# The order of all tasks of a fused threshold attention and quick-GELU kernel, sought anew with other ranks

## The chip, the cores and the metric

The kernel runs on one core of one Trainium2 chip. The metric is the device time of one launch in microseconds, taken as the median of the runs shown.

## The reference

Eight batches of eight heads, 576 positions, 64 values a head; the attention's result is laid out as 4608 tokens of 512 values and goes through a feed-forward block with 2048 hidden values. The two weight matrices come as 64-bit floats, the rest as 32-bit ones.

```python
scores = scale * np.matmul(q, k.transpose(0, 1, 3, 2))
thresh = np.max(scores, axis=-1, keepdims=True) - tau
scores = np.where(scores >= thresh, scores, -1000000000.0)
scores = scores - np.max(scores, axis=-1, keepdims=True)
attn = np.exp(scores)
attn = attn / (np.sum(attn, axis=-1, keepdims=True) + 1e-09)
attn_out = np.matmul(attn, v)
x = attn_out.transpose(0, 2, 1, 3).reshape(B * S, H * D)
h = x @ w_in
g = h * (1.0 / (1.0 + np.exp(-1.702 * h)))
out = (g @ w_out).astype(np.float32)
```

## The kernel before

Two heads of one batch make a pair; there are 32 pairs, n = 0 to 31, and four of them make a batch. The work is cut into named tasks, written (n) or (n, part) below.

For one pair: `load_qk` (L410) and `load_v` (L422) bring q, k and v in through SP's queue. `prep` (L522, DVE) turns q and k. `scores` (L538, PE, nine parts in PSUM), and `keep` (L555, ACT) copies each part to SBUF. `in_groups` (L561, DVE, five parts, the last of half the size) and `over_tiles` (L570) take the maxima; `over_halves` (L581, L594) and `turn_rows` (L605) make one row of limits, which goes to DRAM with `row_out` (L651) and comes back spread over all partitions with `row_in` (L660); pair 2 spreads it on DVE (`spread_max`, L642). `sub` (L666, DVE, five parts), `mask` (L672, ACT) and `exps` (L676, ACT) turn the scores into weights. `values` (L687, PE) multiplies them with v. The sums of the weights are made on PE for pairs 0 to 4 (`sums_by_pe` L687, `one_row` L718, `spread_sums` L770 and L772) and on DVE from pair 5 on (`in_groups` with add, `turn_sums` L744 to L749, then the DRAM trip `sums_out`, `sums_in`). `place_x` (L789, DVE) divides and writes the feed-forward's input xT.

The weights come in 32 pieces of 1 MB, piece 0 to 15 of w_in and 16 to 31 of w_out, each by two transfers on POOL's queue (`load_w`, L473 and L474), one piece after the other. DVE and ACT turn a piece into 32-bit floats by integer work: `cv_ex` (L484, DVE), `cv_power` (L492, ACT), `cv_frac` (L498 and L502, DVE), `cv_end` (L510, DVE). A piece is loaded into one of four corners of the room of w_out or one of two buffers; the next piece for that place is loaded after `cv_end` of the one before. The first load also waits for `hold(3)` (L529), a POOL copy that waits for `prep(3, 1)`.

The feed-forward works on 18 blocks of 256 tokens. Blocks 0 and 1 go together: 32 tasks `mm1_0(j, i)` (L844, PE; j = 0 to 15 slices of the hidden values, i the block), of which slices 4x to 4x+3 need pieces 4x to 4x+3 of w_in, each slice followed by `tanh` (L813, ACT) and `gelu_0` (L850, DVE), which frees one of two PSUM banks; then 32 tasks `mm2(i, p)` (L826, PE), where p = 0 to 7 needs pieces 16+2p and 17+2p. Blocks 2 to 13 take a first product at L804, `gelu` at L816 and a second at L995 by seven products of half size; blocks 14 to 17 do both products so (L909, L995).

What sets the order: nothing in the code's sequence does. Every task is handed to `task(engine, cost, rank, f, ...)`, with the tasks it comes after, the buffers it takes and gives back, and a cost in us. `run_in_order` then plays all of it at build time, engine by engine: an engine that is free takes the ready task of the lowest rank, and the instructions are written in the order in which tasks are taken. The chip runs each engine's list strictly in that order. The rank is the pair's number plus a bias by the kind of task: table EARLY for pairs 0 to 3, SECOND for 4 to 7, LATER for the rest, CV for the weight tasks. FIRST (-9.0) is the rank of the feed-forward's work on ACT, DVE, POOL and SP and of transfers; LAST (1000.0) is that of the feed-forward's products on PE. From pair 7 on, `values` of pair n-2 and `scores` of pair n are bound together, part by part; a pair's scores are let in after every 16th feed-forward task (`gate`).

Of the kernel before, what the change touches and what calls it, by code (L numbers as in the profile page):

```python
# [30 lines left out]
def kernel(  # L31
# [97 lines left out]
    for x in ("raw0", "raw1", "qkT0", "qkT1", "mb"):  # L129
# [3 lines left out]


    EARLY = {
        "exps": -17.61,
        "in_groups": 12.77,
        "keep": 26.48,
        "load_qk": 6.42,
        "load_v": 0.46,  # L140
        "mask": 4.73,
        "one_group": -15.86,
        "one_row": -9.06,
        "over_halves": -11.42,
        "over_tiles": -0.06,
        "place_x": -9.61,
        "prep": -11.56,
        "row_in": 31.26,
        "row_out": -12.68,
        "scores_run": 26.41,  # L150
        "spread_max": 4.27,
        "spread_sums": 4.87,
        "sub": 8.56,
        "sums_by_pe": -5.69,
        "sums_in": 2.27,
        "sums_out": 16.51,
        "turn_rows": -16.86,
        "turn_sums": -5.4,
        "values": 24.67,
        "w_sum": 2.1,  # L160
        "x_sum": -20.63,
    }
    SECOND = {
        "exps": -12.92,
        "in_groups": 29.73,
        "keep": 6.19,
        "load_qk": 1.9,
        "load_v": 13.07,
        "mask": 1.29,
        "one_group": 2.55,  # L170
        "one_row": -2.79,
        "over_halves": -24.79,
        "over_tiles": 9.26,
        "place_x": -19.31,
        "prep": -22.42,
        "row_in": -9.56,
        "row_out": -26.33,
        "scores_run": 2.45,
        "spread_max": 6.39,
        "spread_sums": -1.67,  # L180
        "sub": 27.62,
        "sums_by_pe": 38.88,
        "sums_in": 16.9,
        "sums_out": 8.98,
        "turn_rows": 12.04,
        "turn_sums": -0.33,
        "values": 2.02,
        "w_sum": -3.88,
        "x_sum": -12.22,
    }  # L190
    LATER = {
        "exps": 1.49,
        "in_groups": 1.97,
        "keep": -9.78,
        "load_qk": -5.98,
        "load_v": -3.59,
        "mask": 21.95,
        "one_group": 4.78,
        "one_row": -20.84,
        "over_halves": 8.94,  # L200
        "over_tiles": -3.1,
        "place_x": 4.68,
        "prep": -7.1,
        "row_in": 2.23,
        "row_out": -2.52,
        "scores_run": -13.43,
        "spread_max": -3.68,
        "spread_sums": -27.9,
        "sub": 9.4,
        "sums_by_pe": 4.28,  # L210
        "sums_in": 8.55,
        "sums_out": -0.12,
        "turn_rows": -4.72,
        "turn_sums": 8.12,
        "values": 0.63,
        "w_sum": 21.55,
        "x_sum": 7.65,
    }
    CV = {
        "cv_end": -26.29,  # L220
        "cv_ex": 6.34,
        "cv_frac": -13.49,
        "cv_power": -9.91,
        "load_w": 3.03,
    }

    LAG = {"PE": 0.26, "DVE": 0.18, "ACT": 0.22, "POOL": 0.18, "SP": 0.1}
# [118 lines left out]
    TWICE = ()  # L346
# [728 lines left out]
    SHARED = 0.2 if BY_POOL else 0.0  # L1075
    FFU = 1.727
    T_RANK = FIRST

    W_RANK = (0, 15.75, 22.55, 26.06, 2.06, 16.74)
    ready_w, w_loads, w64 = [], [], 0  # L1080
    for i in range(len(pieces)):
        y = 0 if i < NDC else 2 if i < n_in else 4
        n = NDC if i < NDC else n_in - NDC if i < n_in else n_in
        first = (0, 0, NDC, 0, n_in)[y]
        rank = W_RANK[y] + (W_RANK[y + 1] - W_RANK[y]) * (i - first) / n
        if not wide:
# [12 lines left out]
        over = [ready_w[y] for y in range(i) if i >= n_in and stage(y) == (i - n_in) // PER_STAGE]  # L1099
        ready_w.append(task("DVE", 0.61 + SHARED, rank, cv_end, i, after=[a, m] + over, give=place))  # L1100
# [168 lines left out]
    exped, loaded, summed = {}, {}, {}  # L1269

    def valued(n, pv):

        nonlocal next_blk
        b, hp = divmod(n, NPAIR)
        new = {(b * S + x) // BLK for x in cuts(b)[:-1]} if hp == 0 else set()
        if b:
            new -= {(b * S - 1) // BLK}
        placed[n] = task(
            "DVE", 1.05, float(n), place_x, n, after=[summed[n], pv], take=("xT",) * len(new),
            give=("psA", "rc"),  # L1280
        )
        while hp == NPAIR - 1 and (next_blk + 1) * BLK <= (b + 1) * S:
            if next_blk >= TAIL:
                if (next_blk - TAIL) % 2:
                    two_blocks(next_blk - 1)
            elif next_blk >= PLAIN:
                feed_forward(next_blk)
            elif next_blk == PLAIN - 1:
                first_blocks()
            next_blk += 1  # L1290

    for n in range(NP):
        gate = per_pair * (n - LEAD)
# [38 lines left out]
        if n >= JOINT:  # L1332

            a = None
            for t in range(NKT + 1):
# [4 lines left out]
                    after=exped[m] + [loaded[m], pq, pk] + after if t == 0 else [a],  # L1340
                    take=("psA",) if t == 0 else (), give=(f"v_m{m % 2}",) if t == NKT else (),
# [5 lines left out]
                a = w  # L1347
                for j in js:
# [143 lines left out]
```

## Time and profile before

| what | before |
|---|---|
| time, median of 3 runs | 1314.48 us (1312.47 to 1315.28) |
| profiled execution: span of the instructions | 1309.8 us |
| busy PE | 1260.5 us (96%) |
| busy DVE | 1002.2 us (77%) |
| busy ACT | 646.6 us (49%) |
| DMA, mean over the span | 79 GB/s; 214 GB/s in the first 131 us |

The span runs from the first to the last instruction of one profiled execution; no time of its own is listed for that execution, so the span is set against the runs: 4.7 us of the median lie around it (2.7 of the fastest run, 5.5 of the slowest). Busy times of different engines overlap. Numbers in the page's slices are tenths of 1/40 of the span, 32.7 us each. The traced task times below are read from the instructions of an engine in order, which are the planner's tasks in order.

### The profile page before, as it was taken

Reading aid. Unit: us, or ns where it says so; the run is one execution under the profiler, and the core shown is the slowest. Engines: PE = TensorE matmul, PEld = TensorE weight load, DVE = VectorE, ACT = ScalarE, POOL = GpSimd, SP = SyncE. Lnnn points to the kernel's source line nnn. Section 1 sums busy time; section 2 is a strip of 40 time slices with the busy share of each in tenths; the row PEclk is TensorE's granted clock in tenths of the full one; section 3 lists DMA queues with packets and bytes.
Section 4 is the critical chain, followed back from the end, with each engine's and each line's share of the span. In section 5 each row is a group of like instructions: output and inputs, shape, how many; then the busy total and the mean of one; then the engine's idle time right before and its main releaser. Section 6 shows DMA issues by size and latency. Waiting matters only on the chain. (4 is left out here: it accounts for less than half of the span.)

```text
span 1309.8 us, 22824 instructions
## 1 busy us (share of the span) xinstructions
PE 1260.5 (96%) x9128; PEld 972.6 (74%) x9128; DVE 1002.2 (77%) x1601; ACT 646.6 (49%) x830; POOL 246.1 (19%) x300
## 2 busy tenths in 40 slices
PE   5869999999999999999999999999999999999998
PEld 2436854477688777777778888777777778888887
DVE  7999998989998877778877877777888864652642
ACT  5975656766664544455554545454556540210210
POOL 1301210022030212112020302020212117120120
PEclk8989999999999999999999999999999999999999
DMA  6976967264322222221222222222122110000000
GB/s 118 339 186 214 282 209 132 67 125 83 82 57 71 55 64 64 56 57 44 63 47 61 55 71 55 72 56 70 42 52 54 38 44 9 9 1 33 1 1 32
DMA packets 194309, 103.78 MB, mean 79 GB/s; under 512 B 160284, under 2 KB 171292, under 8 KB 194204
## 3 DMA queue, kind: packets, MB, share of 16 engines
q1 hardware_dynamic: 180476, 64.30, 20.6%
q0 software_dynamic: 11360, 37.74, 9.7%
q8 instruction: 71, 1.16, 0.4%
q10 hardware_dynamic: 2368, 0.30, 0.2%
q14 instruction: 34, 0.28, 0.1%
HBM read 88.40 MB, written 9.70 MB: 75 GB/s over the span
## 5 line engine op out<-in xcount | busy, mean ns | idle before, releaser
L561 DVE TRANSPOSE_TENSOR_REDUCE part<-arena 128x36 f32<-128x1152 f32 x295 | 361.5, 1241 | 45.9 <-ACT arena L555 32.3
L804 PE MATMUL hps<-xT,w_in 128*128 128x256 f32 x1536 | 336.9, 380 | 0.4 <-DVE arena L816 0.4
L804 PEld LDWEIGHTS hps<-xT,w_in 128*128 128x128 f32 x1536 | 290.8, 190 | 45.5 <-issue 5.7
L672 ACT ACTIVATE arena<-arena 128x1152 f32<-128x1152 f32 (+1 forms) x160 | 169.4, 1058 | 144.9 <-DVE arena L666 144.6
L555 ACT COPY arena<-ps 128x576 f32<-128x576 f32 x288 | 170.4, 647 | 121.2 <-PE ps L538 120.9
L666 DVE TENSOR_TENSOR arena<-arena 128x1152 f32<-128x1152 f32 (+1 forms) x158 | 197.5, 1281 | 19.6 <-DMA arena<-row 19.5
L995 PE MATMUL ops<-w_out,arena 128*128 128x256 f32 x896 | 202.9, 381 | 1.2 <-DVE arena L816 1.1
L676 ACT ACTIVATE arena<-arena,shift,scl 128x1152 f32<-128x1152 f32 (+1 forms) x160 | 200.1, 1251 | 4.1
L538 PE MATMUL ps<-arena 64*64 64x288 f32 x2304 | 174.1, 419 | 25.1 <-DVE arena L522 14.4
L995 PEld LDWEIGHTS ops<-w_out,arena 128*128 128x128 f32 x896 | 169.0, 190 | 29.1 <-DVE arena L816 3.7
L961 POOL TENSOR_TENSOR arena<-arena 128x256 f32<-128x256 f32 x56 | 50.8, 907 | 658.4 <-DVE arena L816 556.7
L687 PE MATMUL pv<-arena 64*64 64x288 f32 x2176 | 161.2, 410 | 0.0
L538 PEld LDWEIGHTS ps<-arena 64*64 64x64 f32 x2304 | 83.7, 137 | 93.6 <-ACT arena L555 30.7
L995 PE MATMUL ops<-arena 128*128 128x256 f32 x672 | 150.6, 380 | 0.0
L813 ACT ACTIVATE th<-hps 128x512 f32<-128x512 f32 x112 | 66.0, 589 | 167.9 <-PE hps L804 148.2
L995 PEld LDWEIGHTS ops<-arena 128*128 128x128 f32 x672 | 127.3, 190 | 19.3 <-issue 2.2
L687 PEld LDWEIGHTS pv<-arena 64*64 64x64 f32 x2176 | 82.0, 135 | 55.3 <-issue 12.8
L1017 DVE SCALAR_TENSOR_TENSOR osb<-ops,osb 128x256 f32<-128x256 f32 x98 | 39.5, 414 | 91.8 <-PE ops L995 85.0
L816 DVE SCALAR_TENSOR_TENSOR arena<-th,hps 128x512 f32<-128x512 f32 x96 | 64.1, 667 | 37.1 <-ACT th L813 37.0
L844 PE MATMUL hps<-xT,w_in 128*128 128x256 f32 x256 | 57.3, 382 | 1.3 <-DVE arena L850 1.2
L826 PE MATMUL ops<-w_out,arena 128*128 128x512 f32 x128 | 56.4, 596 | 0.0
L844 PEld LDWEIGHTS hps<-xT,w_in 128*128 128x128 f32 x256 | 48.1, 190 | 11.0 <-DVE arena L850 3.0
(117 smaller groups left out, 1027.8 us busy)
## 6 DMA issues: line engine op xcount, KB each, us to landing
arena<-in_v_dram SPq DMA_DIRECT2D x128, 144.0 KB
arena<-in_q_dram SPq DMA_DIRECT2D x128, 72.0 KB
out_dram<-osb SPq DMA_DIRECT2D x36, 256.0 KB
arena<-in_k_dram SPq DMA_DIRECT2D x124, 72.0 KB
arena<-row SPq DMA_DIRECT2D x62, 144.0 KB
arena<-row_s SPq DMA_DIRECT2D x54, 144.0 KB
w_out<-in_moe_w_in_dram POOLq DMA_DIRECT2D x12, 512.0 KB, 9.4
arena<-in_moe_w_out_dram POOLq DMA_DIRECT2D x12, 512.0 KB, 5.9
```

Source lines behind the costliest of these rows:

```text
L538: nc.tensor.matmul(ps[ts(c, KT), h, 0:SH], lhsT=mats[n, 1][ts(h, D), ts(j, KT)], rhs=mats[n, 0][ts(h, D), ts(c, SH)], start=True, stop=True,)
L555: nc.scalar.copy(out=sT[n, t][:, u], in_=pss.pop((n, j))[:, :, 0:SH])
L561: nc.vector.tensor_reduce(out=stats[n, op][:, t * 2 * QB : min(2 * t + 2, NK) * QB], in_=sT[n, t].rearrange("p u h (g d) -> p (u h g) d", ...
L666: engine.tensor_tensor(out=s, in0=s, in1=mbs[n].unsqueeze(1).to_broadcast(list(s.shape)), op=ALU.subtract)
L672: nc.scalar.activation(out=s, in_=s, func=AF.Prelu, alpha=STEEP)
L676: nc.scalar.activation(out=s, in_=s, func=AF.Exp, scale=scl, bias=shift)
L687: nc.tensor.matmul(o[c][ts(h, D), 0:SH], lhsT=left(j, h)[ts(c, KT)], rhs=sT[n, t][ts(c, KT), u, h, :], start=(j == 0), stop=(j == NK - 1),)
L804: nc.tensor.matmul(hidden[j][:, ts(f, BLK)], lhsT=w_in[:, c, ds((f * HF + j) * P, P)], rhs=xTs[blk][:, c, :], start=(c == 0), stop=(c == N ...
L813: nc.scalar.activation(out=ths[j], in_=hidden[j], func=AF.Tanh, scale=GELU_SCALE / 2)
L816: nc.vector.scalar_tensor_tensor(out=g[:, :, j, :], in0=two(ths.pop(j)), scalar=1.0, in1=two(hidden.pop(j)), op0=ALU.add, op1=ALU.mult,)
L844: nc.tensor.matmul(hidden[j][:, ts(i, BLK)], lhsT=w_in[:, c, ts(j, P)], rhs=xTs[i][:, c, :], start=(c == 0), stop=(c == NDC - 1),)
L995: nc.tensor.matmul(banks[blk][k][:, ts(o, HM)], lhsT=left[:, j, :], rhs=right[:, j, :], start=(j == 0), stop=(j == HF - 1),)
```

## The change

All four bias tables get other values, and far larger ones: before they lie between -28 and +39, after between -55 and +218. Some kinds lose their entry where it isn't used. The bias now reaches tasks whose rank is negative as well (the loads of q and k of pairs 0 and 1), except those of rank FIRST and two tasks by name; before it reached ranks from 0 up. The ranks of the weight loads, W_RANK, change. Four costs that the planner reckons with change: `cv_frac` 0.95 to 1.05, `place_x` 1.05 to 0.9, `over_halves` of pairs that go by DRAM 0.8 to 1.05, `spread_sums` 1.05 to 1.15. No function that emits an instruction is touched.

```diff
     EARLY = {
-        "exps": -17.61,
-        "in_groups": 12.77,
...
-        "values": 24.67,
+        "exps": 142.34,
+        "in_groups": 132.24,
...
+        "values": 115.25,
...
     CV = {
-        "cv_end": -26.29,
-        "cv_ex": 6.34,
-        "cv_frac": -13.49,
-        "cv_power": -9.91,
-        "load_w": 3.03,
+        "cv_end": 53.64,
+        "cv_ex": 114.38,
+        "cv_frac": 162.71,
+        "cv_power": -13.03,
+        "load_w": 14.74,
     }
...
-        if 0 <= rank < LAST:
+        if rank != FIRST and rank < LAST and f not in (first_act, tau_terms):
             biases = EARLY if a[0] < NPAIR else SECOND if a[0] < 2 * NPAIR else LATER
...
-    W_RANK = (0, 15.75, 22.55, 26.06, 2.06, 16.74)
+    W_RANK = (10.13, -10.54, 49.5, -6.3, 43.87, 44.05)
...
-        a = task("DVE", 0.95 + SHARED, rank, cv_frac, i, after=[e])
+        a = task("DVE", 1.05 + SHARED, rank, cv_frac, i, after=[e])
...
-            "DVE", 1.05, float(n), place_x, n, after=[summed[n], pv], take=("xT",) * len(new),
+            "DVE", 0.9, float(n), place_x, n, after=[summed[n], pv], take=("xT",) * len(new),
...
-            "DVE", 1.05 if not quick else 1.3 if n in TWICE else 0.8, r, over_halves, n,
+            "DVE", 1.05 if not quick else 1.3 if n in TWICE else 1.05, r, over_halves, n,
...
-            summed[n] = task("DVE", 1.05, r, spread_sums, n, after=[a], take=("rc",))
+            summed[n] = task("DVE", 1.15, r, spread_sums, n, after=[a], take=("rc",))
```

What the order of the built instructions becomes, beside the order before:

- PE: six of the nine parts of pair 3's scores go between the sums and values of pair 1; the last three parts of pair 5's scores go behind `mm1_0(0, 0)` instead of ahead of it; `values(4)` and its sums go behind `mm1_0(14, 1)` instead of `mm1_0(13, 1)`; the block of `values(5)` and `scores(7)` goes ahead of `mm2(0, 7)` instead of behind `mm2(1, 2)`. From pair 8 on PE's list is the same but for one product of block 12.
- DVE: `prep` of pairs 2 and 3 earlier; `sub(1)` 8.4 us of work later and `sub(2)`, `sub(3)` 8.5 and 8.2 us of work earlier; `cv_end(0)` and `cv_end(1)` from before `sub(1, 2)` and `in_groups(2, 3)` to just ahead of `prep(4, 0)`; the sums of pair 5 and the maxima of pair 6 ahead of `cv_end(31)`.
- SP: the second `load_v` from before `load_qk(2)` to between `row_out(0)` and `row_in(0)`.
- POOL and ACT: the weight loads in the same order; single `keep` and `cv_power` tasks change places with `mask` and `exps`.

More of the change, by code (lines that the diff above doesn't have):

```diff
@@ L135 @@
     EARLY = {
-        "exps": -17.61,
-        "in_groups": 12.77,
[L138 to L158, printed above, removed]
-        "values": 24.67,
-        "w_sum": 2.1,
-        "x_sum": -20.63,
+        "exps": 142.34,
+        "in_groups": 132.24,
+        "keep": 118.26,
+        "load_qk": 114.85,
+        "load_v": 217.78,
+        "mask": 204.23,
+        "one_row": 151.17,
+        "over_halves": 77.78,
+        "over_tiles": 54.81,
+        "place_x": -28.9,
+        "prep": -36.6,
@@ L162 @@
+        "row_in": 119.13,
+        "row_out": 54.38,
+        "scores_run": -9.85,
+        "spread_max": -12.43,
+        "spread_sums": 67.21,
+        "sub": 12.03,
+        "sums_by_pe": -29.14,
+        "turn_rows": 99.41,
+        "values": 115.25,
+        "w_sum": -24.48,
     }
     SECOND = {
[L164 to L189, printed above, removed]
+        "exps": 14.77,
@@ new lines @@
+        "in_groups": 215.43,
+        "keep": 205.66,
+        "load_qk": 49.39,
+        "load_v": 15.49,
+        "mask": 201.87,
+        "one_row": 46.53,
+        "over_halves": 204.6,
+        "over_tiles": 205.68,
+        "place_x": 42.22,
+        "prep": 199.07,
+        "row_in": -16.08,
+        "row_out": -35.4,
+        "scores_run": 100.32,
+        "spread_sums": -22.91,
+        "sub": 212.9,
+        "sums_by_pe": 208.86,
+        "sums_in": -41.96,
+        "sums_out": 204.0,
@@ L190 @@
+        "turn_rows": -55.2,
+        "turn_sums": 98.03,
+        "values": 195.96,
     }
     LATER = {
[L192 to L217, printed above, removed]
+        "exps": 205.54,
+        "in_groups": 204.67,
+        "keep": -17.19,
+        "load_qk": 205.88,
+        "load_v": -16.08,
+        "mask": 217.32,
+        "over_halves": 69.93,
+        "over_tiles": -22.46,
@@ L218 @@
+        "place_x": 116.28,
+        "prep": 152.31,
+        "row_in": -55.43,
+        "row_out": 216.92,
+        "scores_run": -6.53,
+        "sub": 198.53,
+        "sums_in": -13.61,
+        "sums_out": 53.62,
+        "turn_rows": -6.06,
+        "turn_sums": 208.51,
+        "values": 194.66,
+        "x_sum": 204.79,
     }
     CV = {
-        "cv_end": -26.29,
-        "cv_ex": 6.34,
-        "cv_frac": -13.49,
-        "cv_power": -9.91,
-        "load_w": 3.03,
+        "cv_end": 53.64,
```

## The prediction

> **What bounds the kernel now.** I read the page first (busy times, slices), then the chain that ended last, then the windows, then the timelines of PE, DVE, SP and POOL.
>
> ```profile
> span 1309.8 us, 22824 instructions
> ...
> PE 1260.5 (96%) x9128; PEld 972.6 (74%) x9128; DVE 1002.2 (77%) x1601; ACT 646.6 (49%) x830; POOL 246.1 (19%) x300
> ...
> PE 16%; DVE 0%; issue 0%
> ```
>
> PE is busy 96% of the span, and the chain, followed back to 1091 us, is PE alone. The change emits the same instructions (9128 on PE), so the end is the sum of PE's work plus PE's idle time, and only the idle time can move. The windows say where it lies:
>
> ```profile
> core 0: us, PE busy (x) PEld busy (x) DVE busy (x) ACT busy (x) POOL busy (x), PEclk, DMA share, GB/s
> 0.00:131.00 131.00, 93.32 (x1087) 55.77 (x1088) 118.19 (x203) 91.03 (x117) 25.06 (x60) 0.91 0.75 214
> 131.00:262.00 131.00, 126.96 (x867) 75.69 (x869) 121.59 (x196) 84.32 (x105) 16.88 (x27) 0.99 0.66 172
> 262.00:1310.00 1048.00, 1040.26 (x7184) 841.14 (x7172) 762.43 (x1204) 471.23 (x610) 204.15 (x214) 1.00 0.21 51
> ```
>
> Of 49.3 us idle, 37.7 lie in the first 131 us, 4.0 in the next 131, 7.7 in the last 1048 (3.6 of them behind PE's last product). In the first 262 us DVE is busy 240 us; it idles 7.2 us at the start and hardly again, so there DVE is the bound and PE waits for it. The hinge is the first feed-forward product:
>
> ```profile
> 110.27 3.73 PE L538 MATMUL ps<-arena 64*64 64x288 f32 x32 [1.64 <-DVE xT L789]
> 113.93 6.39 PE L844 MATMUL hps<-xT,w_in 128*128 128x256 f32 x28
> ```
> ```profile
> 109.26 0.95 DVE L789 TENSOR_TENSOR xT<-pv,arena 128x256 f32<-128x256 f32 x4
> ```
>
> `place_x(3)` (L789) ends at 110.21; four score tasks then go first, and from 113.93 on PE has work without end. Later idle time is small: 1.2 us behind `gelu_0` (149 to 158), 2.44 us at 246.3 for a `keep`, under 1.1 us each after that.
>
> **The change part by part.** Unit costs are the steps from one start to the next on DVE in the first 400 us: `in_groups` 1.28 (last part 0.76), `sub` 1.30 (0.76), `prep` 0.68, `over_tiles` 0.44, `cv_ex` 0.34, `cv_frac` 1.09, `cv_end` 0.60, `turn_sums` 1.66.
>
> *Steady part and tail: nothing.* From `values(10)` on PE's list differs by one product that changes places with its neighbour, the last 193 feed-forward tasks are the same, and from pair 12 on `exps(n, 4)` stands at the same feed-forward task in both lists, 17 to 23 tasks of about 1.73 us ahead of `values(n)` up to pair 29. DVE and ACT have that cover: they would have to be some 29 us late before PE stood still. ACT and POOL in the tail keep their order but for two neighbours on POOL.
>
> *Work ahead of `place_x(3)`.* Three pieces' `cv_ex`, `cv_frac` and `cv_end` go behind it (3 x 2.03 = 6.1), one `in_groups` of pair 4 comes ahead (1.28): -4.8 us.
>
> *The row of pair 0.* Before, the row has 11.5 us of other DVE work as cover, from `turn_rows(0)` (ends 19.48) to `sub(0, 0)` (30.98). Now both `prep(2)` go ahead of `turn_rows(0)`, so it ends at 20.84, and `sub(0, 0)` is due 2.7 us of work earlier, at 28.3. SP's list decides:
>
> ```profile
> 20.50 2.21 SPq L410 DMA_DIRECT2D arena<-in_q_dram  x4
> 22.80 0.71 SPq L651 DMA_DIRECT2D row<-flat  x2
> 23.56 2.68 SPq L410 DMA_DIRECT2D arena<-in_k_dram  x4
> 26.34 1.24 SPq L660 DMA_DIRECT2D arena<-row  x2
> ```
>
> The last load of k ended its issue at 26.25; with the second `load_v` (2.51) and `row_out(0)` (0.72) now behind it, it ends at 23.0. Then `row_out(0)` to 23.7, `load_v(1)` to 26.2, `row_in(0)` to 27.5. The semaphore counts show that row landing 2.5 us after its issue (27.59 to 30.09), so 30.0 now, and `sub(0, 0)` waits 1.7 us, which DVE has not waited so far. Behind it on DVE stand the other parts of `sub(0)` and the row of pair 1; ACT's `mask(0)` waits for it, and all DVE work up to `place_x(3)` shifts with it. The gain at `place_x(3)` falls to -3.1: it ends at 107.1. The two `load_qk(2)` move up by 2.5 us, so the earlier `prep(2)` find their data (16.6 against 17.0); `prep(3, 1)` ends near 26 instead of 31.06, so POOL's `hold` and the first weight load start 5 us earlier, at about 27.
>
> *First products.* Six of pair 5's score tasks stand between `place_x(3)` and `mm1_0(0, 0)` in the list, but two of three PSUM buffers are free for them earlier, so I take 2 us instead of 3.7: about 109.1. Then three score tasks (1.46) go in front of `mm1_0(0, 1)`: 109.1 + 1.73 + 1.46 = 112.3, against 113.93 + 1.73 + 0.1 = 115.8 now. PE is 3.5 us ahead.
>
> *The last weights, where most of it is given back.* `cv_end(31)` gets 10.55 us more DVE work ahead (six `in_groups` 7.7, one short 0.76, `over_tiles` 0.44, `turn_sums` 1.66). Before, it ended at 197.49, and DVE had lost time to weights not yet landed:
>
> ```profile
> 112.76 0.43 DVE L498 TENSOR_SCALAR w_out<-w_out 128x512 int32<-128x512 int32 x1 [0.82 <-DMA w_out<-in_moe_w_in_dram]
> ...
> 187.91 0.43 DVE L498 TENSOR_SCALAR arena<-arena 128x512 int32<-128x512 int32 x1 [1.51 <-DMA arena<-in_moe_w_out_dram]
> ```
>
> With 1.41 at 143.66 that is 3.7 us. In the new list the work between the `cv_end` that frees a place and the `cv_frac` that needs the next piece grows, for piece 30 from 5.6 to 7.9 us (needed: 187.91 - 180.77 = 7.1) and for piece 20 from 8.2 to 10.8 (needed 9.5), so these waits go. `cv_end(31)`: 197.49 + 10.55 + 1.7 - 3.7 = 206.0. Its user `mm2(0, 7)` now stands behind the block of `values(5)` and `scores(7)`, 9.5 us long (205.25 to 214.76). Before, PE reached `mm2(0, 7)` at 198.25 without the block, so the same point is 207.75. PE could be there at 204.2, but the piece is ready at 206.2: PE waits 2.0 us, with the rest of `mm2` and so `store_0` behind it, and 1.5 us of gain are left. `cv_end(29)` gives the same: 184.20 + 11.16 + 1.7 - 2.2 = 194.9, against `mm2(0, 6)` at 196.5 before.
>
> *The wait at 246.3.* `keep(8, 0)` stands behind the `mask` and `exps` of pair 7 in both ACT lists. DVE's 2.25 us wait for the load ahead of `prep(8, 0)` now has one more `sub` in front (1.30), so ACT is 1.3 us earlier, PE 1.5: the 2.44 us stay.
>
> Two more changes between full and quarter products on PE (65 against 63) cost some 0.1 us each (a start-to-start step of 0.52 instead of 0.43 at 205.25).
>
> **Sum.** Span: -1.5 + 0.2 = -1.3, so about 1308.5; the median stands 4.7 above the span: 1313.2 us. What is below 0.2% (2.6 us) counts as no change, being about what three runs of this kernel spread over.
>
> **Rivals.**
>
> *The front gain stays (faster).* If `sub(0, 0)` finds its row (the DMA engines were 0.80 busy by the windows of the first 16 us and 0.49 in the next 17, so there is room), DVE is 1.7 us earlier throughout, `cv_end(31)` is ready at 204.3, and ACT's chain at 246 comes 3 us earlier. Gain 3.2 to 5: about 1310.4. For it: the costs that the planner now reckons with fit the trace (`spread_sums` 1.15 against 1.17, `cv_frac` 1.05 against 1.09). Against it: `load_v(1)` stands plainly in front of `row_in(0)`.
>
> *The row of pair 1 is late (slower).* Place: `sub(1, 0)`. `turn_rows(1)` now ends at about 37.4 (30.32 + 5.35 + 1.7), inside the stream of the first six weight pieces; before, its row went out at 30.34, ahead of the stream, and yet `row_in(1)`, issued until 33.42, landed at 40.19. `sub(1, 0)` is due at 51.1 (40.97 + 8.43 + 1.7). From below: 0.7 for the issue, 2.0 to land, 1.9 and 6.8 for the way in, 48.8 and no wait. From above: 6.5 for a row out amid weights (172.43 to 178.93, pair 5), and 12.3 for the way in, as long as a load of k took behind weights (90.85 to 103.19): 58.1, a wait of 7 us. I take no wait, since the low end is made of this row's own times. Each us of wait goes on to `cv_end(29)` and `cv_end(31)`: from 1.3 us the gain is gone, from 3.9 the kernel is slower by 0.2%; the upper end gives 1320, the middle of the slow part 1318.
>
> The Trainium skill (DMA: Bandwidth & Descriptors, Queues, rings and completion order) says that each DMA engine takes turns between the queues it has work for, a packet at a time. By that rule a row beside one stream of weights needs about twice its time alone, an estimate of 5.0 instead of 2.5 us, `sub(1, 0)` never waits, and this rival falls away. The trace agrees only in part: 6.8 us for `row_in(1)`, but 12.3 for a load in small packets.
>
> *The list changes and the time does not.* PE in the first 262 us is set by ACT at 246: if `row_in(6)` lands as late as now (220.60, beside a 1 MB transfer by POOL), ACT's chain and all behind it stay, and the result is 1314.5. This lies within my band of no change.
>
> **How the numbers follow.** Forecast with the third rival, within 0.2%: 0.42. Front gain stays: 0.36. Late row, or a like wait at weights or loads: 0.22. The forecast's own range is 1311.9 to 1317.1. The range from 1309.0 to 1318.3 reaches past the middle of either rival and leaves out some 0.09 of the faster end and 0.10 of the slower one.
>
> **What would show it.** Right: `place_x(3)` ends near 107 and the first L844 starts near 109; an idle time of 1 to 2 us on L666 near 28 for a row; PE idle for L510 before L826 near 195 or 206; nothing new after 262 us. Wrong: idle PE of several us before 131 us beyond the 37.7 now, a wait of DVE near 51, or new waits of PE in the steady part.

## The result, and the profile after

The changed kernel takes 1329.43 us (median of 4 runs, 1325.30 to 1331.38), the kernel before 1314.59 in the same session: ratio 1.0111, 95% interval 1.0090 to 1.0131, so 14.8 us slower. The prediction was 1313.2, its range ended at 1318.3. The profiled execution of the changed kernel is its fastest run (1325.3 us); its span is 13.7 us longer than that of before. In every run here the time lies some 1.8 us above the span (1325.3 and 1323.5 us in this one), so the profiled execution of before took some 1311.6 us, an estimate: the 4.7 us under "Time and profile before" are for the most part its distance from the median. Line numbers of the changed kernel are 15 lower than before (`place_x` L774, `sub` L651, `keep` L540, first product L829, the gelu of later blocks L801).

The page (span; busy times; the chain that ended last):

```profile
span 1323.5 us, 22825 instructions
...
PE 1264.6 (96%) x9128; PEld 974.7 (74%) x9128; DVE 1003.3 (76%) x1601; ACT 646.1 (49%) x830; POOL 250.2 (19%) x300
...
PE 69%; DVE 15%; DMA 7%; ACT 4%; issue 3%; SPq 2%; POOL 0%; DVEq 0%; ACTq 0%; POOLq 0%
```

The same 9128 products keep PE busy 4.1 us longer, and PE idles 58.9 us instead of 49.3: both parts are needed for the 13.7. The chain, which before ended in PE's work from 1091 us on, is now followed back to the start, a quarter of it through DVE, DMA and ACT; it names no one place. The windows, cut as in the prediction:

```profile
core 0: us, PE busy (x) PEld busy (x) DVE busy (x) ACT busy (x) POOL busy (x), PEclk, DMA share, GB/s
0.00:131.00 131.00, 92.44 (x1080) 55.58 (x1081) 113.69 (x193) 89.34 (x116) 20.29 (x52) 0.90 0.69 190
131.00:262.00 131.00, 121.05 (x790) 72.95 (x792) 118.38 (x188) 82.48 (x101) 20.57 (x34) 0.97 0.73 192
262.00:1324.00 1062.00, 1051.11 (x7268) 846.20 (x7264) 771.24 (x1222) 474.30 (x614) 209.28 (x214) 1.00 0.21 51
```

PE's idle time rises by 0.9 us in the first window, by 5.9 in the second (131 - 121.05 = 9.95, before 4.04) and by some 3 in the third. DVE, the bound of the first 262 us, is busy 232 us there instead of 240. The hinge, on PE and on DVE:

```profile
110.65 2.19 PE L523 MATMUL ps<-arena 64*64 64x288 f32 x32 [0.90 <-DVE xT L774]
112.77 1.56 PE L829 MATMUL hps<-xT,w_in 128*128 128x256 f32 x6
```
```profile
31.71 2.63 DVE L651 TENSOR_TENSOR arena<-arena 128x1152 f32<-128x1152 f32 x2 [2.69 <-DMA arena<-row]
...
109.59 0.92 DVE L774 TENSOR_TENSOR xT<-pv,arena 128x256 f32<-128x256 f32 x4
...
225.38 2.63 DVE L651 TENSOR_TENSOR arena<-arena 128x1152 f32<-128x1152 f32 x2 [2.01 <-DMA arena<-row]
...
234.77 0.78 DVE L507 STREAM_TRANSPOSE arena<-arena 128x576 f32<-128x576 f32 x1 [4.83 <-DMA arena<-in_k_dram]
```

`place_x(3)` ends at 110.51, no earlier than before (110.21). In brackets stand DVE's waits: 2.69 us for the row of pair 0, then 2.01 for the row of pair 6 and 4.83 for k of pair 8. Before, DVE waited 0.91 and 2.25 us at these two tasks (for the row of pair 6, and for q of pair 8), and from 112 us on no wait of PE was over 2.44:

```profile
220.62 1.36 DVE L666 TENSOR_TENSOR arena<-arena 128x1152 f32<-128x1152 f32 x1 [0.91 <-DMA arena<-row]
224.23 0.78 DVE L522 STREAM_TRANSPOSE arena<-arena 128x576 f32<-128x576 f32 x1 [2.25 <-DMA arena<-in_q_dram]
```
```profile
246.30 1.43 PE L538 MATMUL ps<-arena 64*64 64x288 f32 x16 [2.44 <-ACT arena L555]
```

PE's two long waits in the changed kernel:

```profile
253.77 2.20 PE L523 MATMUL ps<-arena 64*64 64x288 f32 x16 [6.54 <-ACT arena L540]
...
317.32 8.86 PE L789 MATMUL hps<-xT,w_in 128*128 128x256 f32 x32 [3.71 <-DVE arena L801]
```

Where the time goes is read best at the start of the same feed-forward product in both traces. At all points of this table but one PE has the same work behind it; at `mm2(0, 0)` the changed kernel has 24 score products fewer behind it, 1.6 us of work:

| product | before, us | after minus before |
|---|---|---|
| `mm1_0(0, 1)`, first | 115.8 | +0.5 |
| `mm2(0, 0)`, first | 182.6 | -2.3 |
| `mm2`, behind the block of `values(5)` in both | 221.7 | +3.4 |
| `mm2`, behind the wait near 250 | 268.4 | +8.5 |
| block 2, behind the wait at 317 | 340.8 | +12.4 |
| end of the steady part | 1159.2 | +13.7 |

So near 180 PE started this product 2.3 us earlier, and was 0.7 us ahead by equal work. It lost 4.1 in `mm2`, 5.1 near 250, 3.9 by 341 and another 3 in small waits up to 421 (+15.5); from there on the difference changes by less than 2 us. The list of differences under "The change" needs a correction: PE's lists are the same from pair 10 on, not from pair 8. The block of `values(8)` and `scores(10)` stands four products earlier than before (ahead of `mm1(2, 4)`), that of `values(9)` six.

### The profile page after: what moved, and what is told of

The parts are those of the page before. It is cut to its first block, busy times and chain, and to the rows that moved or that the text cites. A ratio compares the mean times of both kernels' runs of the same rounds, so it can differ in the third digit from the quotient of the medians.

```text
span 1323.5 us, 22825 instructions
## 1 busy us (share of the span) xinstructions
PE 1264.6 (96%) x9128; PEld 974.7 (74%) x9128; DVE 1003.3 (76%) x1601; ACT 646.1 (49%) x830; POOL 250.2 (19%) x300
## 4 chain that ended last, share of the span: by engine, by line
PE 69%; DVE 15%; DMA 7%; ACT 4%; issue 3%; SPq 2%; POOL 0%; DVEq 0%; ACTq 0%; POOLq 0%
PE ops L980 23%; PE hps L789 21%; PE pv L672 7%; PE ps L523 7%; PE ps L894 4%; PE ps L980 4%; DVE part L546 3%; DVE arena L651 3%; PE ops L894 3%; DMA arena<-row 2%; ACT arena L661 1%; ACT arena L657 1%; ACT arena L540 1%; DMA arena<-in_k_dram 1%; DVE arena L507 1%
## 5 line engine op out<-in xcount | busy, mean ns | idle before, releaser
L789 PEld LDWEIGHTS hps<-xT,w_in 128*128 128x128 f32 x1536 | 291.9, 191 | 49.4 <-issue 5.7
L540 ACT COPY arena<-ps 128x576 f32<-128x576 f32 x288 | 170.5, 646 | 115.8 <-PE ps L523 115.4
L651 DVE TENSOR_TENSOR arena<-arena 128x1152 f32<-128x1152 f32 (+1 forms) x158 | 198.4, 1301 | 26.8 <-DMA arena<-row 26.7
L946 POOL TENSOR_TENSOR arena<-arena 128x256 f32<-128x256 f32 x56 | 49.3, 881 | 653.6 <-DVE arena L801 551.8
L801 DVE SCALAR_TENSOR_TENSOR arena<-th,hps 128x512 f32<-128x512 f32 x96 | 64.3, 670 | 37.7 <-ACT th L798 37.4
L829 PE MATMUL hps<-xT,w_in 128*128 128x256 f32 x256 | 56.6, 381 | 0.7 <-DVE arena L835 0.7
L959 POOL TENSOR_TENSOR arena<-arena 128x512 f32<-128x512 f32 x28 | 36.0, 1289 | 109.2 <-PE ops L980 109.1
## 6 DMA issues: line engine op xcount, KB each, us to landing
w_out<-in_moe_w_in_dram POOLq DMA_DIRECT2D x12, 512.0 KB, 10.8
```

The lines of the kernel that those rows point to most:

```text
L540: nc.scalar.copy(out=sT[n, t][:, u], in_=pss.pop((n, j))[:, :, 0:SH])
L651: engine.tensor_tensor(out=s, in0=s, in1=mbs[n].unsqueeze(1).to_broadcast(list(s.shape)), op=ALU.subtract)
L789: nc.tensor.matmul(hidden[j][:, ts(f, BLK)], lhsT=w_in[:, c, ds((f * HF + j) * P, P)], rhs=xTs[blk][:, c, :], start=(c == 0), stop=(c == N ...
L801: nc.vector.scalar_tensor_tensor(out=g[:, :, j, :], in0=two(ths.pop(j)), scalar=1.0, in1=two(hidden.pop(j)), op0=ALU.add, op1=ALU.mult,)
```

## Experiments

Theory D: DVE's list and its DMA waits decide, and PE's order ahead of 250 hardly matters. Theory E: PE's own order costs it. For the stretch behind `place_x(7)`, A: the lists there cost by themselves; B: they cost only because everything comes late; C: the front makes the whole loss.

All kernels of this section are the changed kernel with the planner held to a written list for each engine; its costs and the emitted functions stay, and line numbers are 178 higher (L801 is L979, `place_x` L952, `keep` L718):

```diff
+    ORDER = {"PE": [...], "DVE": [...], "ACT": [...], "POOL": [...], "SP": [...]}
...
                     if engine == "PE" and held_for not in (None, i):
                         continue
+                    if engine in ORDER and i != ORDER[engine][at[engine]]:
+                        continue
```

The runs come from several sessions, in which the median of the kernel before lay between 1313.0 and 1314.6 us. The last column sets each kernel against before in its own session; the changed kernel stands at +14.8 by that measure, and the differences in the text go by it.

| kernel | median us | ratio to before | 95% interval | us above before |
|---|---|---|---|---|
| front_new | 1321.62 | 1.0061 | 1.0046 to 1.0076 | +8.1 |
| old_to_mm2_then_new | 1327.34 | 1.0101 | 1.0081 to 1.0121 | +13.9 |
| old_to_p7_then_new | 1322.97 | 1.0074 | 1.0059 to 1.0089 | +9.5 |
| new_to_p7_then_old | 1319.55 | 1.0053 | 1.0036 to 1.0071 | +6.1 |
| after_again | 1329.61 | 1.0110 | 1.0092 to 1.0127 | +16.4 |
| row0_first | 1322.84 | 1.0076 | 1.0061 to 1.0091 | +9.6 |
| hold_later | 1326.92 | 1.0093 | 1.0079 to 1.0107 | +12.9 |
| copies_later | 1322.06 | 1.0073 | 1.0057 to 1.0090 | +8.9 |
| block5_back | 1338.39 | 1.0195 | 1.0170 to 1.0219 | +25.2 |
| block8_back | 1323.49 | 1.0083 | 1.0068 to 1.0098 | +10.3 |
| pe_old_rest_new | 1335.23 | 1.0165 | 1.0149 to 1.0181 | +22.0 |
| gelu4_first | 1327.12 | 1.0094 | 1.0079 to 1.0109 | +13.1 |
| three_repairs | 1318.06 | 1.0030 | 1.0018 to 1.0042 | +4.1 |
| all_gelus_first | 1320.74 | 1.0050 | 1.0033 to 1.0068 | +7.7 |
| new_to_mm2_fixed | 1318.06 | 1.0032 | 1.0019 to 1.0044 | +5.0 |
| before_copy1_later | 1311.83 | 0.9983 | 0.9972 to 0.9993 | -1.4 |
| new_fixed_to_p7 | 1310.88 | 0.9975 | 0.9963 to 0.9987 | -2.3 |

### Where along the list the loss is made

The lists of one kernel up to a task, then those of the other:

```diff
+ front_new:            changed lists until place_x(3) is taken, then the old ones
+ old_to_p7_then_new:   old lists until place_x(7) is taken, then the changed ones
+ new_to_p7_then_old:   changed lists until place_x(7), then the old ones
+ old_to_mm2_then_new:  old lists until mm2(0, 0), then the changed ones
```

front_new: 

> Lists of the changed kernel up to place_x(3), then every engine goes on in the old order. Theory A (the loss is made in two later places: 8.5 us between place_x(3) and the wait at 253, where pair 5 stands ahead of the weights; 5.2 us between 285 and 317, where gelu stands behind pair 9's work): the front costs nothing, since the first feed-forward product starts within 1.2 us of before; 1312 to 1317. Theory B (the second place is only a follow-on of the first): the same, 1312 to 1317. Theory C (the front loses it: DVE had 4.8 us less work ahead of place_x(3) and yet ended 0.3 later, so 5 us of DVE time are lost there and the rest follows): over 1319.

old_to_p7_then_new: 

> Old order up to place_x(7) (near 268 us), then the changed lists. Theory A: the 5.2 us between 285 and 317 belong to the lists there, so 1319 to 1321. Theory B: these 5.2 us come only because DVE and ACT arrive 8 us late; without that lateness nothing is lost: 1313 to 1316. Theory C: as B.

new_to_p7_then_old: 

> Changed lists up to place_x(7) (near 280 us), then the old order. Theory A: the first loss of 8.5 stays and the second of 5.2 goes: 1322 to 1325. Theory B: both stay, since the lateness is the same: 1327 to 1331. Theory C: as B.

old_to_mm2_then_new: 

> Old order up to mm2(0,0) (183 us), then the changed lists: so the weights up to piece 28 are converted as early as before, and what was put ahead of them comes behind. Theory A: the first loss (late weights, then the copies beside the loads of pair 8) goes, the second of 5.2 stays: 1318 to 1321. Theory B: all goes: 1313 to 1316. Theory C: all goes. If the first loss is made behind mm2(0,0), by SP's and DVE's lists there, it stays: 1325 and more.

The lists up to `place_x(7)` cost 6.1 us (1319.55 - 1313.47), below all the alternatives, and those behind it 9.5 (1322.97 - 1313.47), above A's range of 1319 to 1321. B falls: nothing comes late in old_to_p7_then_new, and PE waits all the same (timeline of PE):

```profile
280.45 12.31 PE L967 MATMUL hps<-xT,w_in 128*128 128x256 f32 x48 [2.53 <-ACT osb L996]
...
315.07 8.86 PE L967 MATMUL hps<-xT,w_in 128*128 128x256 f32 x32 [4.21 <-DVE arena L979]
```

That the two figures add up to about the whole 14.8 is in part luck. In the changed kernel's own trace the stretch behind `place_x(7)` costs 5.2 us (from +8.5 to +13.7 in the table of products), in old_to_p7_then_new's 10.3 (from +0.7 to +11.0). The wait at 280 is one that neither kernel has: the changed list puts ACT's copy of the last `mm2` result behind `mask` and `exps` tasks, and in the changed kernel PE comes 8.5 us later and finds the copy done. So A holds in kind, and what the stretch costs depends on how late PE gets there.

The figure for front_new says nothing on C: in the old list the last scores of pair 5 stand ahead of the first product, and with the changed lists up to there they wait 7.30 us for ACT, a wait that neither kernel has. A splice makes waits of its own. old_to_mm2_then_new came out as the last of its alternatives: between `mm2(0, 0)` and `place_x(7)` the changed lists cost 4.4 us more (1327.34 - 1322.97) even with early weights. Its trace has a wait of PE for `keep` of 4.01 us at 199.6, where PE of the changed kernel waits 0.5, so part of this may be the joint's too.

### The row of pair 0

```diff
  row0_first, SP          hold_later, DVE
  row_out(0)              in_groups(1, 2)
- load_v(1)             - prep(3, 1)
  row_in(0)               ...
+ load_v(1)               sub(0, 0)
                        + prep(3, 1)
```

row0_first: 

> The changed kernel, but SP issues the second load_v behind row_in(0) instead of ahead of it. Theory D: sub(0,0) waits 0 to 0.5 instead of 2.7 us, place_x(3) ends near 108 instead of 110.5, and DVE carries 2 us on to the wait at 253: 1326 to 1328. Theory E: the 2 us are lost at mm2(0,6), which waits for cv_end(29) behind loads of weights, or at load_qk(8): 1328 to 1331.

hold_later: 

> The changed kernel with prep(3, 1) moved on DVE from ahead of in_groups(1, 3) to behind sub(0, 0); POOL's first weight load, which waits for it, then goes out near 32 (as in the kernel before) instead of 27, and SP's order is left as it is. If the row of pair 0 is late because it shares the DMA engines with the first weights: it lands 2.3 to 2.7 us after its issue, sub(0,0) waits 0.7 to 1.2 us in place of 1.1 to 6.5, and the time falls by 3 to 6 us with a smaller spread: 1323.5 to 1326.5. If it is late because load_v(1) goes ahead of it: the wait stays at 2.7 and more, 1328 to 1331. If the later weights cost what the row gains: 1328 to 1331 too, with longer waits of DVE for weights.

after_again, the changed kernel once more: 

> The changed kernel as it is, once more beside the three others: 1325 to 1331. Its traces and those of the variants with the same front show sub(0,0) waiting between 1.06 and 2.69 us, so a spread of some us is expected of this order itself.

In after_again's trace the wait that was 2.69 us is 6.53, as DVE, POOL and SP show it:

```profile
35.16 1.36 DVE L651 TENSOR_TENSOR arena<-arena 128x1152 f32<-128x1152 f32 x1 [6.53 <-DMA arena<-row]
```
```profile
26.89 0.56 POOL L458 DMA_DIRECT2D w_out<-in_moe_w_in_dram  x1 [0.31 <-issue]
```
```profile
26.66 1.18 SPq L645 DMA_DIRECT2D arena<-row  x2
```

`row_in(0)` goes out 0.3 us later than in the first trace, but here the first weight load is issued 0.96 us before the row's issue ends (27.85), and the row lands 7.2 us after that. Over the traces with this SP order and early weights the row takes longer, on the whole, the earlier they go: leads of 0.07, 0.08, 0.20, 0.25, 0.28, 0.43 and 0.96 us gave 2.65, 2.6, 3.0, 4.1, 3.4, 4.8 and 7.2 us, and with the weights 0.17 us behind it was 2.5. Only in after_again does the second of the row's two transfers go out (27.30) behind the first weight load (26.89); by the semaphore counts it landed at 33.8 to 35.1, after that load (32.1). In hold_later SP's order is unchanged, the weights go at 33, and the row lands in 2.4:

```profile
30.11 1.36 DVE L829 TENSOR_TENSOR arena<-arena 128x1152 f32<-128x1152 f32 x1 [1.85 <-DMA arena<-row]
...
42.65 0.43 DVE L647 TENSOR_SCALAR w_out<-w_out 128x512 uint32<-128x512 uint32 x1 [2.94 <-DMA w_out<-in_moe_w_in_dram]
```
```profile
33.38 0.56 POOL L636 DMA_DIRECT2D w_out<-in_moe_w_in_dram  x1
```

So two things make DVE wait. The place behind `load_v(1)` alone leaves some 1.2 us: in hold_later DVE waits 1.85, 0.7 of them because `prep(3, 1)` no longer stands in front. What goes beyond that, up to the 6.53, comes with the weights beside the row, and `load_v(1)` is what brings the two together. The time fell by just 1.9 us, within the spread and less than expected, since DVE then waits 2.94 and 1.18 us for the later weights. With the row ahead of `load_v(1)` it goes out at 24.93, and DVE does not wait for it:

```profile
24.93 1.14 SPq L823 DMA_DIRECT2D arena<-row  x2
```
```profile
28.86 3.88 DVE L829 TENSOR_TENSOR arena<-arena 128x1152 f32<-128x1152 f32 x3
```

`place_x(3)` ends at 107.66, against 110.51 and, in after_again, 113.74, and 5.2 us of the loss are gone (9.6 us above before), more than theory D's 2 us, which had been reckoned from the fastest run's wait. So theory C is right for this part of the loss. That the same kernel's row waited 2.69 us in one trace and 6.53 in the other fits the spread of its runs (1325 to 1331).

### The 1 MB copies beside row 6 and the loads of pair 8

```diff
  ACT
- t_minus(0, 0), t_minus(0, 1)   ahead of keep(7, 8)
- t_minus(1, 0), t_minus(1, 1)   ahead of mask(6, 0)
+ t_minus(0, 0), t_minus(0, 1)   ahead of mask(7, 0)
+ t_minus(1, 0), t_minus(1, 1)   ahead of keep(9, 0)
```

> The changed kernel, but on ACT t_minus(0) goes from ahead of keep(7,8) to ahead of mask(7,0), t_minus(1) from ahead of mask(6,0) to ahead of keep(9,0); so POOL's 1 MB copies t_plus(0) and t_plus(1) come some 20 and 35 us later and no longer run beside row_out(6), row_in(6) and load_qk(8). Theory D (up to the wait of 6.5 us at 253 DVE's and ACT's chain decides, and 3.7 of its lateness is DVE's waits of 2.0 for row 6 and 4.8 for load_qk(8, 1) beside these copies): both waits shrink by 3 to 6 us in sum, PE's wait to 1 to 3, the time falls by 4 to 8 us against the changed kernel, to 1321 to 1325. Theory E (PE's order ahead of it decides: the block of values(5) and scores(7) ahead of mm2(0,7)): PE's wait at 253 moves little, 1327 to 1331.

In the changed kernel POOL issues the copies `t_plus(0)` and `t_plus(1)` (9.4 and 9.1 us to land) over the very stretch in which SP moves row 6 and q and k of pair 8:

```profile
213.28 1.61 POOL L940 DMA_DIRECT2D arena<-w_out  x1 [11.68 <-ACT arena L936]
225.06 1.57 POOL L940 DMA_DIRECT2D arena<-w_out  x1 [10.18 <-ACT arena L936]
```
```profile
215.94 1.59 SPq L636 DMA_DIRECT2D row<-flat  x2
221.45 1.12 SPq L645 DMA_DIRECT2D arena<-row  x2
...
224.87 2.81 SPq L395 DMA_DIRECT2D arena<-in_k_dram  x4
```

They come there because `t_minus(0)` waits for `cv_end(31)`, which the new order puts 13.7 us later (211.18 instead of 197.49); before, the first copy was over (199.6 to 209.2) before row 6 left, and only the second ran beside these transfers:

```profile
212.33 1.57 POOL L955 DMA_DIRECT2D arena<-w_out  x1 [11.10 <-ACT arena L951]
```

With the copies later, from copies_later:

```profile
240.28 1.61 POOL L1118 DMA_DIRECT2D arena<-w_out  x1 [36.99 <-ACT arena L1114]
259.81 1.57 POOL L1118 DMA_DIRECT2D arena<-w_out  x1 [17.92 <-ACT arena L1114]
```
```profile
224.83 2.58 DVE L829 TENSOR_TENSOR arena<-arena 128x1152 f32<-128x1152 f32 x2
...
229.26 0.77 DVE L685 STREAM_TRANSPOSE arena<-arena 128x576 f32<-128x576 f32 x1
```
```profile
250.77 1.25 PE L701 MATMUL ps<-arena 64*64 64x288 f32 x16 [1.85 <-ACT arena L718]
```

Neither `sub(6, 0)` nor `prep(8, 1)` waits any more, PE's wait falls from 6.54 to 1.85, and 6.0 us of the loss are gone (8.9 us above before). `row_out(6)` shows the cause at its source: from its issue to that of `row_in(6)`, which waits for it, 5.5 us pass beside the copy (215.94 to 221.45) and 1.2 us without (217.47 to 218.65). That ACT has less work ahead of `mask(6, 0)` is not the gain: in the changed kernel ACT stood idle between `t_minus(1)` and `mask(6, 0)` for 2.02 us, waiting for DVE. Theory D holds. PE still loses 4.7 us of equal work in `mm2` there (at the 221.7 point it is 5.1 us late) and is only 2.8 us late behind the wait: what PE loses ahead of the wait is taken up by it.

block5_back was to undo that loss in `mm2`:

```diff
  PE:  block of values(5) and scores(7) from ahead of mm2(0, 7) to behind mm2(1, 2)
  DVE: cv_* of pieces 28 to 31 from among in_groups(5, add) and in_groups(6) to ahead of most of them
  ACT: cv_power(30), cv_power(31) ahead of keep(7, 0)
```

> The changed kernel, but the block of values(5) and scores(7) stands behind mm2(1,2) again as before, and with it the conversion of pieces 28 to 31 stands ahead of pair 5's last sums on DVE (cv_power(30) and (31) ahead of keep(7,0) on ACT). Theory E: PE no longer loses 5.7 us between mm2(0,0) and mm2(1,4), and the time falls by that: 1322 to 1325. Theory D: PE gets to 247 some 5 us earlier and waits that much longer for keep(8,0), which DVE sets: 1327 to 1331.

It came out at 1338.4, far from both. `place_x(5)` was left where it stood on DVE, and with `values(5)` later DVE waits 10.20 us there. The edit made a larger wait than the one that it was to remove, so theory E was not tested by it; what speaks against E is copies_later.

The same idea on the kernel before, where only `t_plus(1)` ran beside these loads:

```diff
  ACT (old order throughout)
- t_minus(1, 0), t_minus(1, 1)   ahead of keep(7, 4)
+ t_minus(1, 0), t_minus(1, 1)   ahead of keep(9, 0)
```

> The kernel before, only t_minus(1) goes on ACT from ahead of keep(7,4) to ahead of keep(9,0), so the 1 MB copy t_plus(1) runs near 257 instead of beside row_in(6) and load_qk(8) (212 to 222). Theory D (copies beside row 6 and the loads of pair 8 set the wait near 250): DVE's waits of 0.9 and 2.25 us there go, PE's wait of 2.44 at 246 falls to 0 to 0.5, and PE's slow products behind it too: 1310.5 to 1312.5, a little faster than before. If the loads are late for another reason: 1312.5 to 1314.5.

```profile
255.08 1.57 POOL L1118 DMA_DIRECT2D arena<-w_out  x1 [51.87 <-ACT arena L1114]
```
```profile
245.44 1.26 PE L701 MATMUL ps<-arena 64*64 64x288 f32 x16 [0.92 <-ACT arena L718]
```

PE's wait of 2.44 us is 0.92, DVE's waits of 0.91 and 2.25 us are gone, and the kernel is faster than before: ratio 0.9983, interval 0.9972 to 0.9993.

### Behind place_x(7)

The rows of ACT and DVE ahead of PE's wait at 317 in the changed kernel:

```profile
310.40 0.57 ACT L798 ACTIVATE th<-hps 128x512 f32<-128x512 f32 x1
```
```profile
311.88 0.95 DVE L774 TENSOR_TENSOR xT<-pv,arena 128x128 f32<-128x128 f32 x4 [2.35 <-DMA arena<-row_s]
...
316.62 0.65 DVE L801 SCALAR_TENSOR_TENSOR arena<-th,hps 128x512 f32<-128x512 f32 x1
```

The same `gelu(4)` before, 1.4 us behind the end of its `tanh`:

```profile
293.74 0.68 DVE L816 SCALAR_TENSOR_TENSOR arena<-th,hps 128x512 f32<-128x512 f32 x1
```

In the changed kernel `tanh(4)` is done at 310.97, `gelu(4)` comes at 316.62, behind `place_x(8)` (which waits for the row of its sums, not for `values(8)`, as the expectation of gelu4_first below has it) and four more tasks. Four edits:

```diff
+ block8_back: mm1(2, 4), mm1(2, 5) ahead of the block of values(8) on PE, tanh(4), tanh(5) behind tanh(3), gelu(3) to gelu(5) between the parts of sub(9)
+ pe_old_rest_new: old lists up to place_x(7), then only PE's old list
+ gelu4_first: gelu(4) ahead of place_x(8) on DVE
+ all_gelus_first: gelu4_first, gelu(5) to gelu(7) earlier, and the repairs of row0_first and copies_later
```

block8_back: 

> The changed kernel, but slices 4 and 5 of block 2's first product stand ahead of the block of values(8) and scores(10) on PE again, tanh(4) and tanh(5) ahead of keep(10,0) on ACT, gelu(3) to gelu(5) ahead of or between the parts of sub(9) on DVE. If the loss of 9.5 us behind place_x(7) is that block's place (gelu(4) behind tanh(4) behind the block's last keeps, a wait of 3.7 us, and 1.7 more since PE's next 24 products take 6.97 instead of 5.28 us): the time falls by 4 to 6 us, to 1323 to 1326. If it is the order of the work on DVE (sub(9) and place_x(8) ahead of gelu(4)) whatever PE's place: it falls by less than 2.

pe_old_rest_new: 

> Old order up to place_x(7); from there PE's old list, the other engines' new lists. If PE's earlier blocks of values(8) and values(9) make the loss of 9.5 us that old_to_p7_then_new showed: 1313 to 1316. If DVE's and ACT's lists make it (gelu and tanh behind the work of pairs 8 to 10): 1319 to 1323, PE waiting for a gelu between 275 and 320.

gelu4_first: 

> The changed kernel with one DVE task moved: gelu(4) of block 2 from behind place_x(8), prep(11, 0), prep(11, 1), in_groups(9, 1) and in_groups(9, 2) to ahead of them. If DVE's order is the cause of the last loss: DVE now idles 2.4 to 3.1 us ahead of place_x(8), which waits for values(8), while tanh(4) is done 1 to 2 us before; so gelu(4) costs DVE nothing there, PE's wait of 3.7 to 4.4 us near 313 to 321 goes, the slow products behind it too (1.7): 4.5 to 6 us below the changed kernel, 1323.5 to 1325.5. If PE then waits as long for the next gelu or for ACT (as it did when the block was moved back): less than 2 us below, 1327.5 to 1330.

all_gelus_first: 

> As three_repairs, and on DVE gelu(5), gelu(6) and gelu(7) of block 2 earlier too: behind prep(11, 1), in_groups(9, 2) and in_groups(9, 3), each about where its tanh is done. In three_repairs PE still waited 3.1 us near 311, then for gelu(5), with 1.7 of slow products behind it. If the place of the gelus on DVE is the whole rest of the loss: that wait is under 1 us, the time 1312 to 1315. If ACT's list (tanh behind masks and exps of pair 9) holds them as well: PE waits 2 to 4 us there still, 1316 to 1319.

PE's longest wait behind `place_x(7)`, in the order block8_back, gelu4_first, all_gelus_first (one row from PE's timeline of each):

```profile
321.91 3.37 PE L1158 MATMUL ops<-w_out,arena 128*128 128x256 f32 x8 [3.99 <-DVE arena L979]
```
```profile
318.49 5.41 PE L967 MATMUL hps<-xT,w_in 128*128 128x256 f32 x16 [2.60 <-DVE arena L979]
```
```profile
357.12 3.50 PE L967 MATMUL hps<-xT,w_in 128*128 128x256 f32 x10 [3.94 <-DVE osb L1180]
```

Each edit removed its wait and a like one came up next: at the second products, at `gelu(5)`, and at DVE's additions at 357. block8_back came out in the range of its first alternative (1323 to 1326), but not for its reason: of the 4.5 us that it gains (10.3 above before) its trace shows 0.6 in this stretch up to 347. Its row of pair 0 waited 1.56 us, and PE was 2.2 us further at `mm2(0, 0)`; the rest isn't resolved. gelu4_first gains 1.7 us, between its alternatives and within the spread, and all_gelus_first, 7.7 us above before and beyond both its alternatives, is no faster than three_repairs (4.1), which lacks its last three moves. PE's old list with the other engines' new ones came out at 1335.2, far above both alternatives (PE waits of 2.4 to 6.0 us up to 367): like block5_back it made larger waits than it was to remove, so it does not tell whether PE's earlier blocks have a part in the loss. What is shown is that the lists behind `place_x(7)` cost PE 5.2 us in the changed kernel's trace, and 10.3 where PE comes there in time. That DVE's and ACT's lists make it is what the waits say; it is not shown by an edit, and which of their tasks would have to move was not found.

### The causes together

three_repairs (row0_first, copies_later and gelu4_first at once): 

> The changed kernel with three moves at once: load_v(1) behind row_in(0) on SP; t_minus(0) and t_minus(1) later on ACT (their copies away from row 6 and load_qk(8)); gelu(4) ahead of place_x(8) on DVE. If these three are the whole loss and add up (-6.3 and -7.2 as measured alone, some -5 for the third): 1310 to 1313, no slower than the kernel before. If something else of the new order costs: 1315 and more.

new_fixed_to_p7 (row0_first and copies_later, old lists behind `place_x(7)`): 

> The changed order up to place_x(7) with both repairs (copies t_plus(0), t_plus(1) later; load_v(1) behind row_in(0)), then the old order. Theory D: the three losses that were found are out, what stays is DVE's waits for weights between 110 and 190 and the products that wait for cv_end(29): 1311 to 1315, 5 to 8 us below new_to_p7_then_old. If the losses do not add up like this: 1316 to 1320.

new_to_mm2_fixed (changed lists with row0_first up to `mm2(0, 0)`, then old ones with `t_minus(1)` later): 

> A try at a faster version: the changed order up to mm2(0,0) with load_v(1) behind row_in(0), then the old order with t_minus(1) ahead of keep(9,0). If the new front's 2 to 4 us on PE at mm2(0,0) last, since the old order behind it has no block ahead of mm2(0,7): 1307 to 1311. If the weights, some 13 us later than in the old order, make mm2 wait: 1313 to 1320.

three_repairs takes back 10.8 of the 14.8 us and stays 4.1 us slower than before: the three are not the whole. With the old lists behind `place_x(7)` instead of the moved `gelu(4)` the time is 1310.9, 2.3 us below before and so faster than both kernels; PE's longest wait after `place_x(3)` is the one near 250, and it has no long one behind it:

```profile
251.30 1.26 PE L701 MATMUL ps<-arena 64*64 64x288 f32 x16 [1.85 <-ACT arena L718]
```

So the way from new_fixed_to_p7 up to the changed kernel, 17.1 us, is 10.8 for the row, the copies and the first `gelu`, and 6.4 for the rest of the lists behind `place_x(7)` (with rounding). Other orders of the same edits would split it in another way, since one loss hides part of the next. The third run answers little: PE waits 10.49 us at the joint (191), as in front_new.

## Why the prediction was wrong, by its steps

*The front.* The step that failed is the term "that row landing 2.5 us after its issue", taken from a run in which the weights started 4.7 us behind the row's issue. Two sentences further on the text itself moves the first weight load to 27, on top of the row's issue (26.3 to 27.5), and does not price it. It landed in 2.5 to 7.2 us; `sub(0, 0)` waited 0.70 to 6.53 instead of 1.7. The rest of that sum was 2 us or more too good: without the wait `place_x(3)` was to end at 105.4 and ended at 107.66 in row0_first, at 110.47 in new_fixed_to_p7. Waits that the sum put at nothing are part of it: DVE waited for ACT's `keep` (1.2 and 1.4 us between 66 and 76) and, in new_fixed_to_p7, 3.1 us for weights.

*The rival of the late row* had the right mechanism, a row inside the weights' stream, at the wrong pair: `sub(1, 0)` did not wait (its row landed at 50.89, due 52.41). By the rule of the Trainium skill (DMA: Bandwidth & Descriptors, Queues, rings and completion order) a row beside weights was to take 5.0 us, an estimate. The traces agree up to 4.8; the 7.2 us in after_again do not fit it.

*The last weights.* The mechanism, conversions that push PE's `mm2`, was right, and both sizes were off: `cv_end(31)` came at 211.18, not 206.0, mostly because `place_x(3)` was 3.4 us later than predicted and the waits for weights that were to "go" did not (0.87, 0.70 and 1.33 us). By equal work PE fell from 0.7 us ahead to 3.4 behind, a loss of 4.1 where 2.0 were to be given back.

*The wait at 246.* "ACT is 1.3 us earlier, PE 1.5: the 2.44 us stay": the wait became 6.54. I moved `cv_end(31)` by 8.5 us and did not follow its users, `t_minus` on ACT and `t_plus` on POOL, although my last rival names a "1 MB transfer by POOL" beside `row_in(6)`. This term was missing, not mis-sized; copies_later prices it at 6.0 us.

*The steady part: nothing.* Right from 421 on, where the cover of 17 to 23 feed-forward tasks was counted (from pair 12). Between `place_x(7)` and there I counted no cover and took the lists for the same. They aren't, for pairs 8 and 9 and the gelus among them: 5.2 us in the changed kernel's trace and 9.5 by old_to_p7_then_new, with no equal term in any of the rivals.

*The price of a wait.* Each was priced at its length. A wait of PE over 2.4 us mostly costs more than that, by the clock: 1.7 us at the wait of 3.71 (below).

## What to carry over

When a step moves, follow all that is released by it to the end of its queue, the transfers above all: here a conversion moved by 14 us dragged a 1 MB copy onto a row and a load that stood untouched in their lists. A transfer's time from a trace holds only with the neighbours that it had there, so look for what else is issued within a microsecond of it in the new order. "The lists are the same" has to be counted from the last wait of PE, not from where it is convenient.

## What the runs showed of the hardware

After a long wait PE runs at half its clock (windows of the changed kernel, the wait and the 3.8 us behind it, twice; PEclk is the third number from the end):

```profile
247.30:253.70 6.40, 0.00 (x0) 0.00 (x0) 6.19 (x14) 6.33 (x8) 0.00 (x0) 0.91 0.11 42
253.80:257.60 3.80, 3.80 (x32) 2.00 (x36) 3.80 (x4) 3.08 (x5) 0.00 (x0) 0.50 0.28 78
...
313.60:317.30 3.70, 0.01 (x1) 0.00 (x0) 3.70 (x5) 1.62 (x3) 0.00 (x0) 1.00 0.01 2
317.30:321.20 3.90, 3.88 (x10) 3.10 (x11) 3.87 (x5) 0.00 (x0) 0.72 (x1) 0.56 0.00 0
```

The 24 products behind the second wait take 6.97 us; behind waits of 0.7 to 1.1 us they take 5.28. Over the traces of all kernels here, between 112 and 700 us, 33 of 35 waits of 2.42 us or more were followed by a granted clock of 0.50 to 0.66 over the next 3.8 us, and 30 of 34 waits of 0.9 to 1.91 us by 1.00. The two exceptions among the long ones (2.56 and 3.79 us, both in pe_old_rest_new) were followed by 1.00, so the length alone does not decide. Of the 4.1 us that PE was busy longer for the same products, 1.7 are these 24. Most of the rest, 2.9 us, lies in the products that sum the weights of pairs 0 to 3, in the first 112 us (24.8 instead of 21.9 us); the mean granted clock was 0.88 there instead of 0.90, and that it makes the 2.9 is not shown. The Trainium skill (TensorE: Matmul & The Clock Gate, Why this matters for your kernels) warns of idle gaps of more than some 3 us; here 2.42 was enough in two traces.
